# Token-mixing weights by row block, and a shorter pipeline for the first batch, in a fused retention and token-mixing kernel

## The chip, the cores and the metric

The kernel runs on one core of one Trainium2 chip. The metric is device time in microseconds. The core has five engines with an instruction stream each: TensorE (PE; its weight loads are listed as PEld), VectorE (DVE), ScalarE (ACT), GpSimd (POOL) and SyncE (SP, which only issues DMAs here). An engine works through its own stream in order and waits for others through semaphores.

## The reference

A retention recurrence over 8 heads, then a layer that mixes tokens with a phase and channels with a matrix:

```python
# q, k, v: [4, 8, 768, 64]
for t in range(S):
    state = gamma * state + outer(k[:, :, t], v[:, :, t])
    y[:, :, t] = scale * (q[:, :, t] @ state)
x = y with heads joined                      # [4, 768, 512]
theta = x @ w_theta
zr, zi = x * cos(theta), x * sin(theta)
u = x + w_tok_r @ zr + w_tok_i @ zi          # over the 768 tokens of a batch
out = u + maximum(u @ w_ch, 0)
```

All inputs and the output are float32; the two w_tok matrices are 768x768, w_theta and w_ch 512x512.

## The kernel before, in words

Tokens are cut into blocks of 128: six per batch, 24 chunks in all (number n = 6 * batch + c). The matmuls run in bf16. All code is emitted in one order by hand, and each engine takes its instructions in that order.

A chunk goes through these steps:

- **load_chunk** (L73): three DMAs on SP's queue, k, v, q, 256 KB each, into buffers kf, vf, qf (8 each).
- **att_prep** (L138, POOL): cast k to kb, scale q to qb and v to vb by powers of gamma.
- **T**, att_T (L151): eight PE transposes into kq_ps; DVE copies them to kqT.
- **A**, att_A (L162): eight PE matmuls k by q into at_ps; DVE multiplies by the causal mask into at.
- **Y**, att_Y (L180): PE matmuls of the running state with q (L186, for c > 0) and of at with vb (L192) into yT_ps, and the state update st_ps (L200, for c < 5). ACT copies yT_ps to xT and the state to stbd.
- **X**, att_X (L215): PE transposes xT back (x_ps, copied by DVE to x_sb) and multiplies by w_theta (th_ps, L226); ACT takes cosine and sine into cs.
- **Z**, att_Z (L234): DVE multiplies cs with x_sb into z.

A token block m of a batch needs z of all six chunks of that batch:

- **M**, moe_M (L241): twelve 512-wide matmuls of the transposed token weights wT with z into y_ps, in two halves; after the second, DVE adds x_sb into u.
- **U**, moe_U (L256): four transposes of u, which ACT copies to uT.
- **O**, moe_O (L264): four 512-wide matmuls with w_ch into o_ps, DVE's final maximum and sum into ot, and the output DMA on SP's queue.

The weights are prepared on the way: w_theta is cast by ACT (wth), w_ch by POOL (wch), and **w_tok** (L274) takes one block of 128 rows of w_tok_r or w_tok_i: a cast on POOL to wrow (3 buffers), six PE transposes into w_ps, and a copy into wT by DVE or ACT. There are twelve such blocks.

PSUM holds at_ps (two banks), st_ps (one), three buffers "acc" that yT_ps, th_ps, y_ps and o_ps take in turn, and two buffers "tr" that kq_ps, x_ps, u_ps and w_ps take in turn. A taker waits until the buffer's previous content has been copied out.

The order is a table of slots (L287 to L302). Chunk n starts in slot tau[n] and passes T, A, Y, X, Z in five successive slots, so five chunks are in flight. The chunks of batches 1 to 3 start three slots later than their number. Block m has M in slot mu[m], the first four slots after T of its batch's last chunk, and U and O in the slot behind. Within a slot the order is: loads, w_tok, att_prep of the next chunk, T, Z, U, first half of M, A, O, second half of M, Y, X (L304 to L344). The w_tok loads (L91, six buffers) are issued in slot 2, all of w_tok_r, then w_ch, then all of w_tok_i, ahead of the loads of chunk 6; the twelve w_tok run in slots 5 to 8, three per slot.

Of the kernel before, what the change touches and what calls it, by code (L numbers as in the profile page):

```python
# [14 lines left out]
FT = mybir.dt.float32  # L15
BF = mybir.dt.bfloat16
# [16 lines left out]
def kernel(  # L33
# [17 lines left out]
    nc = tc.nc  # L51
    B, H, S, D = q.shape
    dm = H * D
    P = 128
    nT = S // P
    nD = dm // P
# [3 lines left out]
    NCH = B * nT  # L60
# [11 lines left out]

    def load_chunk(n):  # L73
        b, c = divmod(n, nT)
        for name, src in (("kf", k), ("vf", v), ("qf", q)):
            t = io.tile([P, H, D], FT, name=name, bufs=8)
            nc.sync.dma_start(  # L77
                out=t, in_=src[b, :, c * P:(c + 1) * P, :].rearrange("h s d -> s h d"))
            raw[n, name] = t

    wdma = {}

    def load_w512(name, src):
        t = io.tile([P, nD, dm], FT, name="w512", bufs=1)
        nc.sync.dma_start(out=t, in_=src.rearrange("(a p) e -> p a e", p=P))
        wdma[name] = t

    def load_wtok(r, t0):
        src = (moe_w_tok_r, moe_w_tok_i)[r]
        t = io.tile([P, S], FT, name="wtok", bufs=6)  # L90
        nc.sync.dma_start(out=t, in_=src[t0 * P:(t0 + 1) * P, :])  # L91
        wdma[r, t0] = t

    load_chunk(0)
    load_chunk(1)
    load_w512("th", moe_w_theta)
    for n in range(2, 6):
        load_chunk(n)


    posn = const.tile([P, nT], FT)
# [17 lines left out]
    ident = const.tile([P, P], BF)  # L119
# [6 lines left out]
    for i in range(2):  # L126
        t = const.tile([P, NP, P], BF, name=f"stbd{i}")
# [3 lines left out]
    wth = const.tile([P, nD, dm], BF)  # L131
    wch = const.tile([P, nD, dm], BF)
# [5 lines left out]
    def att_prep(n):  # L138
        c = n % nT
        r3 = "p (h d) -> p h d"  # L140
        kb = work.tile([P, dm], BF, name="kb", bufs=4)
        qb = work.tile([P, dm], BF, name="qb", bufs=3)
        vb = work.tile([P, dm], BF, name="vb", bufs=4)
        nc.gpsimd.tensor_copy(kb.rearrange(r3, h=H), raw[n, "kf"])  # L144
        nc.gpsimd.tensor_mul(qb.rearrange(r3, h=H), raw[n, "qf"],  # L145
                             _bcast_last(qsc[:, c], D))
        nc.gpsimd.tensor_mul(vb.rearrange(r3, h=H), raw[n, "vf"],  # L147
                             _bcast_last(vsc[:, c], D))
        st[n] = dict(kb=kb, qb=qb, vb=vb)

    def att_T(n):  # L151
        s = st[n]
        kq_ps = psum.tile([P, 2 * NP, P], BF, name="kq_ps", tag="tr", bufs=2)
        for i, src in enumerate((s["kb"], s["qb"])):
            for j in range(NP):
                nc.tensor.transpose(kq_ps[:, i * NP + j, :],  # L156
                                    src[:, j * P:(j + 1) * P], ident)
        kqT = work.tile([P, 2 * NP, P], BF, name="kqT", bufs=4)
        nc.vector.tensor_copy(kqT, kq_ps)  # L159
        s["kqT"] = kqT  # L160

    def att_A(n):  # L162
        s = st[n]
        kqT = s["kqT"]
        at_ps = psum.tile([P, 2, NP, P], FT, name="at_ps", tag="at", bufs=1)
        for j in range(NP):
            for par in range(2):
                rows = slice(par * D, (par + 1) * D)
                nc.tensor.matmul(at_ps[:, par, j, :], kqT[rows, j, :],  # L169
                                 kqT[rows, NP + j, :], start=(j == 0),  # L170
                                 stop=(j == NP - 1), skip_group_check=True)
        at = work.tile([P, 2, NP, P], BF, name="at", bufs=2)
        nc.vector.tensor_mul(at.rearrange("p a j t -> p (a j) t"),  # L173
                             at_ps.rearrange("p a j t -> p (a j) t"),
                             _bcast_mid(mask, H))
        s["at"] = at
# [57 lines left out]
    def att_Z(n):  # L234
        b, c = divmod(n, nT)
        nc.vector.tensor_mul(zs[b][:, c], st[n]["cs"], _bcast_mid(xs[b][:, c, :], 2))  # L236
# [1 line left out]

    mo = {}

    def moe_M(m, half):  # L241
        b, t0 = divmod(m, nT)
        if half == 0:
            mo[m] = dict(y=psum.tile([P, dm], FT, name="y_ps", tag="acc", bufs=3))
        y_ps = mo[m]["y"]
        for s0 in range(half * 3, half * 3 + 3):
            for r in range(2):
                nc.tensor.matmul(y_ps, wT[r][:, s0, t0 * P:(t0 + 1) * P],  # L248
                                 zs[b][:, s0, r, :], start=(s0 == 0 and r == 0),
                                 stop=(s0 == nT - 1 and r == 1))  # L250
        if half == 1:
            u = work.tile([P, dm], BF, name="u", bufs=3)
            nc.vector.tensor_add(u, y_ps, xs[b][:, t0, :])  # L253
            mo[m]["u"] = u

    def moe_U(m):  # L256
        u_ps = psum.tile([P, nD, P], BF, name="u_ps", tag="tr", bufs=2)
        for j in range(nD):
            nc.tensor.transpose(u_ps[:, j, :], mo[m]["u"][:, j * P:(j + 1) * P], ident)  # L259
        uT = work.tile([P, nD, P], BF, name="uT", bufs=2)  # L260
        nc.scalar.copy(uT, u_ps)  # L261
        mo[m]["uT"] = uT

    def moe_O(m):  # L264
        b, t0 = divmod(m, nT)
        o_ps = psum.tile([P, dm], FT, name="o_ps", tag="acc", bufs=3)
        for j in range(nD):
            nc.tensor.matmul(o_ps, mo[m]["uT"][:, j, :], wch[:, j, :], start=(j == 0),  # L268
                             stop=(j == nD - 1))
        ot = work.tile([P, dm], FT, name="ot", bufs=4)  # L270
        nc.vector.scalar_tensor_tensor(ot, o_ps, 0.0, mo[m]["u"], ALU.max, ALU.add)  # L271
        nc.sync.dma_start(out=out[b, t0 * P:(t0 + 1) * P, :], in_=ot)

    def w_tok(r, t0):  # L274
        row = work.tile([P, S], BF, name="wrow", bufs=3)
        nc.gpsimd.tensor_copy(row, wdma[r, t0])
        w_ps = psum.tile([P, nT, P], BF, name="w_ps", tag="tr", bufs=2)
        for s0 in range(nT):
            nc.tensor.transpose(w_ps[:, s0, :], row[:, s0 * P:(s0 + 1) * P], ident)
        dst = wT[r][:, :, t0 * P:(t0 + 1) * P]  # L280
        if t0 % 2:
            nc.scalar.copy(dst, w_ps)
        else:
            nc.vector.tensor_copy(dst, w_ps)


    tau = {}  # L287
    for n in range(NCH):
        tau[n] = n if n < nT else n + 3
    mu = {}  # L290
    for m in range(B * nT):
        b = m // nT
        ready = tau[b * nT + nT - 1] + 4
        mu[m] = max(ready, mu.get(m - 1, 0) + 1)
    stage = {}
    for n in range(NCH):
        for off, f in enumerate("TAYXZ"):
            stage[f, tau[n] + off] = n
    for m in range(B * nT):
        stage["M", mu[m]] = m  # L300
        stage["O", mu[m] + 1] = m
    last = mu[B * nT - 1] + 1  # L302

    att_prep(0)  # L304
    for slot in range(last + 1):
        g = lambda f: stage.get((f, slot))
        if slot == 0:
            nc.scalar.copy(wth, wdma["th"])
        if slot == 2:
            for r in range(2):  # L310
                for t0 in range(nT):
                    load_wtok(r, t0)
                if r == 0:
                    load_w512("ch", moe_w_ch)
            for n in range(6, 8):
                load_chunk(n)
        if slot == 7:
            nc.gpsimd.tensor_copy(wch, wdma["ch"])
        if slot > 2 and slot + 5 < NCH:
            load_chunk(slot + 5)  # L320
        if 5 <= slot < 9:
            for i in range((slot - 5) * 3, (slot - 4) * 3):
                w_tok(i // nT, i % nT)
        nxt = stage.get(("T", slot + 1))
        if nxt is not None:
            att_prep(nxt)
        if g("T") is not None:
            att_T(g("T"))
        if g("Z") is not None:
            att_Z(g("Z"))  # L330
        if g("O") is not None:
            moe_U(g("O"))
        if g("M") is not None:
            moe_M(g("M"), 0)
        if g("A") is not None:
            att_A(g("A"))
        if g("O") is not None:
            moe_O(g("O"))
        if g("M") is not None:
            moe_M(g("M"), 1)  # L340
        if g("Y") is not None:
            att_Y(g("Y"))
        if g("X") is not None:
            att_X(g("X"))  # L344


# [28 lines left out]
```

## Time and profile before

| | before |
|---|---|
| time, median of 3 runs | 202.91 us (202.55 to 203.26) |
| profiled execution: time | 203.53 us |
| profiled execution: span | 201.8 us |
| PE busy | 168.5 us (83%) |
| PEld busy | 94.9 us (47%) |
| DVE busy | 108.7 us (54%) |
| ACT busy | 79.0 us (39%) |
| POOL busy | 78.9 us (39%) |

Two numbers need care. A PE matmul row lists the whole passage of a matmul through the array (379 ns for a 512-wide one), while successive ones start about 216 ns apart; so work on PE is counted from start to start. And shares of busy time are means over stages that have different limits. The span begins with the first instruction and ends with the last.

### The profile page before, as it was taken

Reading aid. Unit: us, or ns where it says so; the run is one execution under the profiler, and the core shown is the slowest. Engines: PE = TensorE matmul, PEld = TensorE weight load, DVE = VectorE, ACT = ScalarE, POOL = GpSimd, SP = SyncE. Lnnn points to the kernel's source line nnn. Section 1 sums busy time; section 2 is a strip of 40 time slices with the busy share of each in tenths; the row PEclk is TensorE's granted clock in tenths of the full one; section 3 lists DMA queues with packets and bytes.
Section 4 is the critical chain, followed back from the end, with each engine's and each line's share of the span. In section 5 each row is a group of like instructions: output and inputs, shape, how many; then the busy total and the mean of one; then the engine's idle time right before and its main releaser. Section 6 shows DMA issues by size and latency. Waiting matters only on the chain.

```text
span 201.8 us, 3699 instructions
## 1 busy us (share of the span) xinstructions
PE 168.5 (83%) x1456; PEld 94.9 (47%) x1480; DVE 108.7 (54%) x153; ACT 79.0 (39%) x147; POOL 78.9 (39%) x105
## 2 busy tenths in 40 slices
PE   0235786898999999799999999999999999877872
PEld 0123544665445655565565555555555444333330
DVE  1133453775565677679667766676557434233221
ACT  3031482687113433576543454335544343111110
POOL 4555859689855427585536452225000000000000
PEclk9999998799999999999999999999999999999999
DMA  6999999999999999999999111100111001112111
GB/s 143 245 284 218 221 356 394 400 203 233 220 175 229 221 213 255 253 258 260 231 228 235 61 52 55 52 28 27 52 55 52 28 25 55 52 62 83 64 52 52
DMA packets 81137, 32.22 MB, mean 160 GB/s; under 512 B 75488, under 2 KB 75488, under 8 KB 81120
## 3 DMA queue, kind: packets, MB, share of 16 engines
q1 hardware_dynamic: 81120, 31.99, 68.7%
q8 instruction: 11, 0.18, 0.4%
q14 instruction: 6, 0.05, 0.1%
HBM read 25.69 MB, written 6.29 MB: 158 GB/s over the span
## 4 chain that ended last, share of the span: by engine, by line
PE 70%; SPq 10%; ACT 5%; DVE 5%; DMA 3%; issue 3%; POOL 2%; ACTq 0%; POOLq 0%
PE y_ps L248 29%; PE o_ps L268 11%; SPq L77 10%; PE th_ps L226 9%; PE yT_ps L192 4%; PE kq_ps L156 3%; DMA qf<-in_q_dram 3%; PE at_ps L169 3%; PE u_ps L259 3%; DVE u L253 3%; PE st_ps L200 3%; PE x_ps L223 3%; PE yT_ps L186 2%; ACT cs L231 2%; ACT cs L230 1%
## 5 line engine op out<-in xcount | busy, mean ns | idle before, releaser
L248 PE MATMUL y_ps<-z,wti 128*128 128x512 bf16 x144 | 54.6, 379 | 0.9
L248 PE MATMUL y_ps<-z,wtr 128*128 128x512 bf16 x127 | 48.1, 379 | 0.0
L206 ACT CAST xT<-yT_ps 128x512 bf16<-128x512 f32 x24 | 14.1, 586 | 62.8 <-PE yT_ps L192 62.7
L159 DVE COPY kqT<-kq_ps 128x1024 bf16<-128x1024 bf16 x24 | 16.6, 690 | 30.1 <-PE kq_ps L156 30.1
L173 DVE TENSOR_TENSOR at<-at_ps,mask 128x1024 bf16<-128x1024 f32 x24 | 29.3, 1221 | 6.4 <-PE at_ps L169 6.4
L147 POOL TENSOR_TENSOR vb<-vf,vsc 128x512 bf16<-128x512 f32 x24 | 26.4, 1099 | 13.9 <-PE st_ps L200 7.8
L145 POOL TENSOR_TENSOR qb<-qf,qsc 128x512 bf16<-128x512 f32 x24 | 25.0, 1043 | 12.6 <-DMA qf<-in_q_dram 12.6
L144 POOL CAST kb<-kf 128x512 bf16<-128x512 f32 x24 | 15.8, 657 | 30.0 <-PE st_ps L200 26.4
L268 PE MATMUL o_ps<-wch,uT 128*128 128x512 bf16 x94 | 24.4, 381 | 2.9 <-ACT uT L261 2.7
L271 DVE SCALAR_TENSOR_TENSOR ot<-o_ps,u 128x512 f32<-128x512 f32 x24 | 16.5, 685 | 18.6 <-PE o_ps L268 18.2
L261 ACT COPY uT<-u_ps 128x512 bf16<-128x512 bf16 x24 | 14.1, 586 | 31.4 <-PE u_ps L259 31.4
L226 PE MATMUL th_ps<-wth,xT 128*128 128x512 bf16 x91 | 24.3, 388 | 0.7 <-issue 0.4
L236 DVE TENSOR_TENSOR z<-cs,x_sb 128x1024 bf16<-128x1024 bf16 x24 | 18.7, 781 | 8.8 <-ACT cs L231 8.7
L253 DVE TENSOR_TENSOR u<-y_ps,x_sb 128x512 bf16<-128x512 f32 x24 | 16.6, 692 | 11.3 <-PE y_ps L248 11.2
L248 PEld LDWEIGHTS <-wtr 128*128 128x128 bf16 x144 | 14.1, 98 | 14.1
L248 PEld LDWEIGHTS <-wti 128*128 128x128 bf16 x144 | 14.1, 98 | 14.0
L230 ACT ACTIVATE cs<-th_ps,halfpi 128x512 bf16<-128x512 f32 x24 | 16.5, 687 | 10.5 <-PE th_ps L226 10.4
L156 PE MATMUL kq_ps<-ident,kb 128*128 128x128 bf16 x96 | 10.4, 238 | 8.2 <-POOL kb L144 8.0
L156 PE MATMUL kq_ps<-ident,qb 128*128 128x128 bf16 x96 | 10.6, 241 | 6.9 <-POOL qb L145 6.9
L231 ACT ACTIVATE cs<-th_ps,zerob 128x512 bf16<-128x512 f32 x24 | 16.3, 680 | 0.0
L211 ACT CAST stbd<-st_ps 64x256 bf16<-64x256 f32 x40 | 14.7, 366 | 0.4
L156 PEld LDWEIGHTS <-kb 128*128 128x128 bf16 x96 | 7.8, 106 | 13.4 <-POOL kb L144 8.6
(44 smaller groups left out, 165.4 us busy)
## 6 DMA issues: line engine op xcount, KB each, us to landing
kf<-in_k_dram SPq DMA_DIRECT2D x24, 256.0 KB, 4.8
vf<-in_v_dram SPq DMA_DIRECT2D x24, 256.0 KB, 5.1
qf<-in_q_dram SPq DMA_DIRECT2D x24, 256.0 KB, 5.2
out_dram<-ot SPq DMA_DIRECT2D x24, 256.0 KB, 2.0
wtok<-in_moe_w_tok_r_dram SPq DMA_DIRECT2D x6, 384.0 KB, 6.6
wtok<-in_moe_w_tok_i_dram SPq DMA_DIRECT2D x6, 384.0 KB, 7.1
w<-in_moe_w_theta_dram SPq DMA_DIRECT2D x1, 1024.0 KB, 6.6
w<-in_moe_w_ch_dram SPq DMA_DIRECT2D x1, 1024.0 KB, 9.3
```

What stands on the lines that cost most here:

```text
L77: nc.sync.dma_start(out=t, in_=src[b, :, c * P:(c + 1) * P, :].rearrange("h s d -> s h d"))
L145: nc.gpsimd.tensor_mul(qb.rearrange(r3, h=H), raw[n, "qf"], _bcast_last(qsc[:, c], D))
L147: nc.gpsimd.tensor_mul(vb.rearrange(r3, h=H), raw[n, "vf"], _bcast_last(vsc[:, c], D))
L156: nc.tensor.transpose(kq_ps[:, i * NP + j, :], src[:, j * P:(j + 1) * P], ident)
L173: nc.vector.tensor_mul(at.rearrange("p a j t -> p (a j) t"), at_ps.rearrange("p a j t -> p (a j) t"), _bcast_mid(mask, H))
L226: nc.tensor.matmul(th_ps, s["xT"][:, j, :], wth[:, j, :], start=(j == 0), stop=(j == NP - 1))
L230: nc.scalar.activation(cs[:, 0, :], th_ps, AF.Sin, bias=halfpi, scale=1.0)
L231: nc.scalar.activation(cs[:, 1, :], th_ps, AF.Sin, bias=zerob, scale=1.0)
L236: nc.vector.tensor_mul(zs[b][:, c], st[n]["cs"], _bcast_mid(xs[b][:, c, :], 2))
L248: nc.tensor.matmul(y_ps, wT[r][:, s0, t0 * P:(t0 + 1) * P], zs[b][:, s0, r, :], start=(s0 == 0 and r == 0), stop=(s0 == nT - 1 and r == 1))
L253: nc.vector.tensor_add(u, y_ps, xs[b][:, t0, :])
L268: nc.tensor.matmul(o_ps, mo[m]["uT"][:, j, :], wch[:, j, :], start=(j == 0), stop=(j == nD - 1))
```

## The change

The table of slots goes. The program is written as a part for the six chunks of batch 0 and a loop for the rest.

- Loads: within a chunk q goes before v. kf, qf, vf have nine buffers, w512 two, wtok four. Behind the loads of chunks 0 to 5 come row block 0 of both token weights, w_ch, chunk 6, and then in turn a pair of row blocks (1 to 5) and a chunk (7 to 11), then chunk 12.
- w_tok now takes a pair, the real and the imaginary block t0; DVE copies the real one, ACT the imaginary one. Pair 0 stands behind the six chunks of batch 0, pair m + 1 in the slot of block m.
- The pipeline is shorter: Y of a chunk follows A in the same slot, X one slot later, Z two slots later. In batch 0 the order of an iteration is T(n), Y(n-1), A(n), X(n-1), Z(n-2).
- M of block 0 starts ahead of Y and X of chunk 5. Blocks of batch 0 then run in the slots of chunks 6 to 11, the slot of chunk 12 has no M, and blocks from 6 on run in the slots of chunks 13 and up.
- Within a slot: loads, T, Z, att_prep, first half of M, U of the block before, A, second half of M, O of the block before, Y, w_tok, X.

```diff
-        for name, src in (("kf", k), ("vf", v), ("qf", q)):
-            t = io.tile([P, H, D], FT, name=name, bufs=8)
+        for name, src in (("kf", k), ("qf", q), ("vf", v)):
+            t = io.tile([P, H, D], FT, name=name, bufs=9)
...
-        t = io.tile([P, nD, dm], FT, name="w512", bufs=1)
+        t = io.tile([P, nD, dm], FT, name="w512", bufs=2)
...
-        t = io.tile([P, S], FT, name="wtok", bufs=6)
+        t = io.tile([P, S], FT, name="wtok", bufs=4)
...
-    for n in range(2, 6):
+    for n in range(2, nT):
         load_chunk(n)
+    load_wtok(0, 0)
+    load_wtok(1, 0)
+    load_w512("ch", moe_w_ch)
+    load_chunk(nT)
+    for t0 in range(1, nT):
+        load_wtok(0, t0)
+        load_wtok(1, t0)
+        load_chunk(nT + t0)
+    load_chunk(2 * nT)
...
-    def w_tok(r, t0):
...
+    def w_tok(t0):
+        for r in range(2):
+            row = work.tile([P, S], BF, name="wrow", bufs=3)
+            nc.gpsimd.tensor_copy(row, wdma[r, t0])
+            w_ps = psum.tile([P, nT, P], BF, name="w_ps", tag="tr", bufs=2)
+            for s0 in range(nT):
+                nc.tensor.transpose(w_ps[:, s0, :], row[:, s0 * P:(s0 + 1) * P], ident)
+            dst = wT[r][:, :, t0 * P:(t0 + 1) * P]
+            if r:
+                nc.scalar.copy(dst, w_ps)
+            else:
+                nc.vector.tensor_copy(dst, w_ps)
...
+    for n in range(nT):
+        att_T(n)
+        if n == 1:
             nc.scalar.copy(wth, wdma["th"])
+        if n > 0:
+            att_Y(n - 1)
+        att_A(n)
+        if n > 0:
+            att_X(n - 1)
+        if n > 1:
+            att_Z(n - 2)
+        if n + 1 < nT:
+            att_prep(n + 1)
+    w_tok(0)
+    nc.gpsimd.tensor_copy(wch, wdma["ch"])
+    att_Z(nT - 2)
+    moe_M(0, 0, 3)
+    att_Y(nT - 1)
+    att_X(nT - 1)
+    att_Z(nT - 1)
...
+    for i, (n, m) in enumerate(slots):
+        if n is not None and n + 5 < NCH and n >= nT + 2:
+            load_chunk(n + 5)
+        if n is not None:
+            att_T(n)
+        if prev2 is not None:
+            att_Z(prev2)
+        if i + 1 < len(slots) and slots[i + 1][0] is not None:
+            att_prep(slots[i + 1][0])
+        if m is not None and m > 0:
+            moe_M(m, 0, 3)
+        if prev_m is not None:
+            moe_U(prev_m)
+        if n is not None:
+            att_A(n)
+        if m is not None:
+            moe_M(m, 3, nT)
+        if prev_m is not None:
+            moe_O(prev_m)
+        if n is not None:
+            att_Y(n)
+        if m is not None and m + 1 < nT:
+            w_tok(m + 1)
+        if prev_n is not None:
+            att_X(prev_n)
+        prev2, prev_n, prev_m = prev_n, n, m
+    moe_U(prev_m)
+    moe_O(prev_m)
```

Three places in the order of the engines' streams. First SP's queue behind the loads of chunk 5, before:

```order
L91 DMA wtok<-in_moe_w_tok_r_dram 128x768 x6
L85 DMA w_213<-in_moe_w_ch_dram 128x4x512
L91 DMA wtok<-in_moe_w_tok_i_dram 128x768 x6
L77 DMA kf<-in_k_dram 128x8x64
L77 DMA vf<-in_v_dram 128x8x64
```

and now:

```order
L91 DMA wtok<-in_moe_w_tok_r_dram 128x768
L91 DMA wtok<-in_moe_w_tok_i_dram 128x768
L85 DMA w_114<-in_moe_w_ch_dram 128x4x512
L77 DMA kf<-in_k_dram 128x8x64
L77 DMA qf<-in_q_dram 128x8x64
L77 DMA vf<-in_v_dram 128x8x64
L91 DMA wtok<-in_moe_w_tok_r_dram 128x768
L91 DMA wtok<-in_moe_w_tok_i_dram 128x768
L77 DMA kf<-in_k_dram 128x8x64
```

Two row blocks instead of twelve stand ahead of chunk 6, and one chunk follows each pair.

Second VectorE's stream around M of block 0 (wtr is wT of the real weights). Before, from Z of chunk 5 on (z from cs_724):

```order
L159 COPY kqT_748<-kq_ps_739 128x1024
L236 TENSOR_TENSOR z_341<-cs_724,x_sb_340 128x1024
L253 TENSOR_TENSOR u_764<-y_ps_751,x_sb_340 128x512
L159 COPY kqT_787<-kq_ps_778 128x1024
L173 TENSOR_TENSOR at_812<-at_ps_803,mask_138 128x1024
```

and now, from the copy of block 0 on (z from cs_560 is chunk 4, from cs_619 chunk 5; kqT_638 is chunk 6; u_663 belongs to block 0):

```order
L294 COPY wtr_215<-w_ps_566 128x6x128
L245 TENSOR_TENSOR z_293<-cs_560,x_sb_292 128x1024
L237 COPY x_sb_292<-x_ps_608 128x512
L245 TENSOR_TENSOR z_293<-cs_619,x_sb_292 128x1024
L168 COPY kqT_638<-kq_ps_629 128x1024
L182 TENSOR_TENSOR at_655<-at_ps_646,mask_206 128x1024
L262 TENSOR_TENSOR u_663<-y_ps_586,x_sb_292 128x512
L294 COPY wtr_215<-w_ps_685 128x6x128
```

Z of chunk 5 has moved ahead of the copy kqT of chunk 6, and the mask product of chunk 6 stands between Z and u.

Third TensorE's stream in the last blocks, where no attention is left. Before, from the end of a block's M (y_ps_2565) on:

```order
L248 MATMUL y_ps_2565<-z_2058,wti_148 128x512
L259 LDWEIGHTS u_2586
L259 MATMUL u_ps_2588<-ident_133,u_2586 128x128
...
L248 LDWEIGHTS wtr_147
L248 MATMUL y_ps_2595<-z_2058,wtr_147 128x512
```

and now, from the end of the first half of the last block's M (y_ps_2588) on; u_2578 belongs to the block before it, so its u stands six matmuls back:

```order
L257 MATMUL y_ps_2588<-z_2013,wti_216 128x512
L268 LDWEIGHTS u_2578
L268 MATMUL u_ps_2595<-ident_201,u_2578 128x128
...
L257 LDWEIGHTS wtr_215
L257 MATMUL y_ps_2588<-z_2013,wtr_215 128x512
```

U of a block stood directly behind that block's M, and stands now behind the first half of the next block's M.

More of the change, by code (lines that the diff above doesn't have):

```diff
@@ L239, with moe_M @@
     mo = {}
-    def moe_M(m, half):
+    def moe_M(m, lo, hi):
         b, t0 = divmod(m, nT)
-        if half == 0:
+        if lo == 0:
             mo[m] = dict(y=psum.tile([P, dm], FT, name="y_ps", tag="acc", bufs=3))
         y_ps = mo[m]["y"]
-        for s0 in range(half * 3, half * 3 + 3):
+        for s0 in range(lo, hi):
             for r in range(2):
@@ L250, in moe_M @@
                                  stop=(s0 == nT - 1 and r == 1))
-        if half == 1:
+        if hi == nT:
             u = work.tile([P, dm], BF, name="u", bufs=3)
@@ L272, in moe_O @@
         nc.sync.dma_start(out=out[b, t0 * P:(t0 + 1) * P, :], in_=ot)
-    def w_tok(r, t0):
[L275 to L284, printed above, removed]
@@ L287 @@
[L287 to L302, printed above, removed]
+    def w_tok(t0):
[10 more added lines that the diff above has]
+                nc.vector.tensor_copy(dst, w_ps)
@@ L304 @@
     att_prep(0)
-    for slot in range(last + 1):
-        g = lambda f: stage.get((f, slot))
-        if slot == 0:
+    for n in range(nT):
+        att_T(n)
+        if n == 1:
             nc.scalar.copy(wth, wdma["th"])
[L309 to L344, printed above, removed]
@@ new lines @@
+        if n > 0:
[14 more added lines that the diff above has]
+    att_Z(nT - 1)
+    slots = []
+    m = 0
+    for n in range(nT, NCH + 2):
+        b, c = divmod(n, nT)
+        slots.append((n if n < NCH else None,
+                      None if n == 2 * nT else m))
+        m += slots[-1][1] is not None
@@ new lines @@
+    while m < B * nT:
+        slots.append((None, m))
+        m += 1
+    prev_n, prev_m, prev2 = None, None, None
+    att_prep(nT)
+    for i, (n, m) in enumerate(slots):
[24 more added lines that the diff above has]
+        prev2, prev_n, prev_m = prev_n, n, m
```

## The prediction

> **What bounds the kernel now.** I read the page first, then stages of it, then the rows of TensorE.
>
> ```profile
> span 201.8 us, 3699 instructions
> PE   0235786898999999799999999999999999877872
> GB/s 143 245 284 218 221 356 394 400 203 233 220 175 229 221 213 255 253 258 260 231 228 235 61 52 55 52 28 27 52 55 52 28 25 55 52 62 83 64 52 52
> ```
>
> The profiled execution took 203.53 us, so 1.7 us lie around its span of 201.8. TensorE (PE) is thin in the first ten slices, full in the middle, thin again in the last six. What the change is worth stands in those two ends. The middle is TensorE's own pace, as one slot (chunk and token block side by side) shows:
>
> ```profile
> 111.48 0.39 PE L156 MATMUL kq_ps<-ident,kb 128*128 128x128 bf16 x4
> 111.93 0.39 PE L259 MATMUL u_ps<-ident,u 128*128 128x128 bf16 x4
> 113.55 0.40 PE L169 MATMUL at_ps<-kqT 64*128 64x128 bf16 x8
> 113.88 1.04 PE L268 MATMUL o_ps<-wch,uT 128*128 128x512 bf16 x4
> 114.75 0.38 PE L248 MATMUL y_ps<-z,wtr 128*128 128x512 bf16 x1
> 116.04 0.39 PE L186 MATMUL yT_ps<-kqT,stbd 128*128 128x128 bf16 x4
> 116.71 0.40 PE L200 MATMUL st_ps<-vb,kb 128*128 128x128 bf16 x4
> 116.94 0.39 PE L223 MATMUL x_ps<-ident,xT 128*128 128x128 bf16 x4
> 118.03 0.39 PE L156 MATMUL kq_ps<-ident,kb 128*128 128x128 bf16 x4
> ```
>
> The first column is the start, and no row names an idle time. From start to start: T (the L156 transposes) 0.45, U and the first half of M 1.62, A 0.33, O 0.87, the second half of M 1.29, Y 0.67 and its state update 0.23, X 1.09. Together 118.03 - 111.48 = 6.55 us. Reordering within such a slot can gain nothing.
>
> At the back end there is a hole:
>
> ```profile
> 166.00:202.00 36.00, 26.23 (x138) 11.50 (x137) 10.85 (x17) 5.26 (x9) 0.00 (x0) 0.99 0.16 59
> 177.38 0.40 PE L259 MATMUL u_ps<-ident,u 128*128 128x128 bf16 x4 [0.79 <-DVE u L253]
> 178.91 1.03 PE L268 MATMUL o_ps<-wch,uT 128*128 128x512 bf16 x4
> 180.85 0.38 PE L248 MATMUL y_ps<-z,wti 128*128 128x512 bf16 x1
> 182.02 0.40 PE L259 MATMUL u_ps<-ident,u 128*128 128x128 bf16 x4 [0.79 <-DVE u L253]
> 195.18 0.69 DVE L253 TENSOR_TENSOR u<-y_ps,x_sb 128x512 bf16<-128x512 f32 x1 [0.60 <-PE y_ps L248]
> ```
>
> In the stage 166 to 202 PE is busy 26.2 of 36 us. A block without attention takes 182.02 - 177.38 = 4.64 us, but its work ends at 180.85 plus one 512-wide pace of 0.22, so it is 3.69 us. The other 0.95 us is U's wait for VectorE's u (0.69 us long).
>
> At the front end PE waits for data:
>
> ```profile
> 20.70 1.33 SPq L77 DMA_DIRECT2D vf<-in_v_dram  x1
> 22.07 1.14 SPq L77 DMA_DIRECT2D qf<-in_q_dram  x1
> 35.81 0.43 SPq L77 DMA_DIRECT2D kf<-in_k_dram  x1
> 28.67 1.04 POOL L145 TENSOR_TENSOR qb<-qf,qsc 128x512 bf16<-128x512 f32 x1 [2.40 <-DMA qf<-in_q_dram]
> 30.66 4.75 POOL L276 CAST wrow<-wtok 128x768 bf16<-128x768 f32 x6
> 37.20 1.90 POOL L318 CAST wch<-w 128x2048 bf16<-128x2048 f32 x1 [1.80 <-DMA w<-in_moe_w_ch_dram]
> 49.27 0.38 PE L248 MATMUL y_ps<-z,wtr 128*128 128x512 bf16 x1
> ```
>
> Chunk 5 is complete only at 28.67, chunk 6 is not even asked for until 35.81, because all twelve w_tok loads stand before it in SP's queue, and the first token-mixing matmul runs at 49.27.
>
> **The change, stage 1: up to T of chunk 7.** Loads up to chunk 5 are the same bytes; only q now goes ahead of v, one issue step (22.07 - 20.70 = 1.4 us) sooner. Chunk 5's qb is then ready between 28.4 and the old 29.7. But PE has more behind it by then: in the new order T of chunk 5 stands behind A of chunk 4, Y of 3 and X of 2 and 3, 0.33 + 0.90 + 2 x 1.09 = 3.4 us that before came later. I put that T's end at 29.4, with 28.6 and 31 as ends.
>
> From there the chain is one of short waits. The durations:
>
> ```profile
> L206 ACT CAST xT<-yT_ps 128x512 bf16<-128x512 f32 x24 | 14.1, 586 | 62.8 <-PE yT_ps L192 62.7
> L230 ACT ACTIVATE cs<-th_ps,halfpi 128x512 bf16<-128x512 f32 x24 | 16.5, 687 | 10.5 <-PE th_ps L226 10.4
> L231 ACT ACTIVATE cs<-th_ps,zerob 128x512 bf16<-128x512 f32 x24 | 16.3, 680 | 0.0
> L282 ACT COPY wti<-w_ps 128x768 bf16<-128x768 bf16 x3 | 2.3, 806 | 0.0
> L159 DVE COPY kqT<-kq_ps 128x1024 bf16<-128x1024 bf16 x24 | 16.6, 690 | 30.1 <-PE kq_ps L156 30.1
> L236 DVE TENSOR_TENSOR z<-cs,x_sb 128x1024 bf16<-128x1024 bf16 x24 | 18.7, 781 | 8.8 <-ACT cs L231 8.7
> L173 DVE TENSOR_TENSOR at<-at_ps,mask 128x1024 bf16<-128x1024 f32 x24 | 29.3, 1221 | 6.4 <-PE at_ps L169 6.4
> ```
>
> - Y of chunk 4 to 30.3, A of 5 to 30.65, X of 4 (behind xT, 0.59) 30.8 to 31.9. The two row blocks' transposes, twice 0.33, to 32.6; their casts on POOL (0.8 each, 4.75 / 6) follow vb of chunk 5 and are done by 31.4.
> - On ACT the copy of the imaginary block stands behind both cs of chunk 4: 31.95 + 1.27 + 0.80 = 34.0. M(0), first half: to 35.15. Y of 5 to 35.8, wait for xT 0.65, X of 5 to 37.55, T of 6 to 38.0.
> - A of chunk 6 now waits longest: on VectorE kqT of 6 stands behind z of 5, which waits for cs of 5: 37.6 + 1.27, z 0.8, kqT 0.69, so 40.45; A to 40.8, M(0) second half to 42.1.
> - Y of 6 takes the accumulator buffer of M(0), so it waits for u (0.69): 42.85 to 43.4. Block 1's transposes to 44.2 (below).
>
> **Clock.** These waits leave PE mostly idle from 38.0 to 40.45, and before shows what may follow:
>
> ```profile
> 20.00:22.00 2.00, 0.98 (x12) 0.63 (x12) 0.17 (x1) 0.51 (x2) 1.92 (x2) 1.00 1.38 218
> 30.00:32.00 2.00, 0.46 (x6) 0.34 (x6) 0.00 (x0) 0.79 (x2) 2.00 (x3) 1.00 1.03 402
> 34.00:36.00 2.00, 2.00 (x26) 1.30 (x23) 1.66 (x4) 0.00 (x0) 1.40 (x2) 0.50 1.05 398
> 36.00:38.00 2.00, 1.78 (x15) 1.32 (x13) 1.50 (x2) 1.32 (x3) 0.80 (x1) 0.65 1.04 402
> ```
>
> The seventh number after the times is the granted clock: after PE was busy 0.46 of 2 us, it was 0.50 and 0.65 in the next busy stages, that is half rate for 2 + 1.4 = 3.4 us, a loss of 1.7 us of work. I charge 1.4 (part falls into waits), with 0 and 3.4 (twice over) as ends. [...] T of chunk 7 then starts at 44.2 + 1.4 = 45.6.
>
> **Do data arrive?** By the rates above (218 GB/s for chunks of 0.786 MB, 402 for whole rows): bytes up to chunk 5 are in by 26 to 28.5, then two row blocks, w_ch, chunk 6 at about 34.5 (wch's cast, 1.9 us, and chunk 6's three on POOL, 2.7 us, end by 37.7), blocks 1 by 37, chunk 7 at 41. POOL finishes vb of 7 at 42.1 and the two casts at 43.8, just ahead of PE: the 44.2 above. Per later slot 0.786 + 0.786 + 0.262 MB (the output) take at those rates 3.6 + 2.0 + 1.2 = 6.8 us against 7.55 us of PE. SP is held at pair 3 until POOL has cast pair 1, and the chunk loads queue behind it; that loop spans two slots, its issue (4.2) + landing (about 5) + POOL's five operations (4.4) make 13.6, or 6.8 us per slot. Both fit, by 0.7 us.
>
> **Stage 2: slots of chunks 7 to 23.** 17 x 6.55 = 111.4. Added: four pairs of block transposes, 4 x 0.66, each with about 0.35 us until VectorE's copy frees the buffer for X, 4.0 in all; 0.4 once for block 1's copy. Taken off: slot 12 has no M (2.6), slot 13 no U and O (1.1), chunk 5 of three batches no state update (0.7), chunk 0 of two no L186 (0.6). Slot 12 without M has little cover: A waits 0.5 for kqT, Y 0.4 for at. Sum 111.7: to 157.3.
>
> **Stage 3: tail.** U of the block before now stands behind the next first half of M (1.29 us), which covers u (0.69), and O behind the second half, which covers uT (0.59). Seven blocks at 3.69 and one X: 26.9, to 184.2. After the last M (its u starts at 195.18, 0.2 behind it) before needed 201.8 - 195.0 = 6.8 us; O of block 22 (0.86) now lies inside that. End 184.2 - 0.9 + 6.8 = 190.1, with the 1.7 around it 191.8. The profiled run is 0.6 above the median of the three, so 191.2 on that scale.
>
> As a check: when T of chunk 7 starts, 4.4 us of block transposes are still owed but A and Y of 6 (0.9) are done; before, that T began 2.6 us after 49.27. The front gives only 51.9 + 0.9 - 45.6 - 4.4 = 2.8 us. The rest, 8.9, is holes closed later, mostly in the tail. The front is the unsure part, the tail is not.
>
> **Rivals.**
> 1. The change doesn't do what it says at the front: the transposes are only moved, and the new waits (A of 6, Y of 6, block copies) eat the 2.8 us. 194.0. For it: the chain above is nearly all waits. Against: two of them are short by count. 0.15.
> 2. The clock stays at half from T of 5 to T of 7. That is 9.3 us of PE work by the steps above; doubled, and less the 1.4 charged, 199.1. For it: the 0.50 row. Against: the same rows show it back after 3.4 us of busy PE. 0.10.
> 3. Loads set the pace in slots 6 to 11. If rows go no faster than chunks (218 GB/s throughout), 1.835 MB take 8.4 us, 6 x 0.87 more: 196.4. 0.10. The same mechanism ends **slower** where the rate falls under 193 GB/s: then a slot takes 9.5 us and six of them give back the 11.7. At 175, the lowest slice of the GB/s row while loads run (the first apart), a slot takes 10.5 and the end is 209. For it: in-order SP, four buffers, PE's transposes standing ahead of X. Against: that slice had no queue of loads. 0.03.
>
> **How the numbers follow.** Forecast 191.2, chance 0.62. Range 187.5 to 198: below, T of chunk 5 at its early end, no clock loss, and a block's copies free; above, rivals 1 and the first form of 3. A measurement here tells about 0.3% from no change. Faster 0.95 (all but the slower form and a fifth of rival 2), same 0.02, slower 0.03.
>
> **What would show it.** First token-mixing matmul near 34 instead of 49.27; T of chunk 7 between 44 and 47; slots of 7.5 then 6.55 us; tail blocks of 3.7 us without a wait for u. T of 7 later than 50, or slots 8 to 11 above 8 us with POOL waiting for wtok, would make the prediction wrong.

## The result and the profile after

| | before | after |
|---|---|---|
| time, median of 4 runs | 202.73 us (202.33 to 203.26) | 193.57 us (192.85 to 196.05) |
| ratio to before, 95% interval | 1 | 0.9544 (0.9498 to 0.9591) |
| profiled execution: time, span | 203.53 us, 201.8 us | 194.15 us, 192.4 us |

The run of 196.05 us was a disturbed one; the ratio leaves it out. The time falls by 9.2 us, where 11.7 were forecast. The page of after, with the rows of its slices (each 4.8 us):

```profile
span 192.4 us, 3717 instructions
PE 167.3 (87%) x1480; PEld 95.1 (49%) x1480; DVE 113.1 (59%) x153; ACT 80.2 (42%) x147; POOL 82.4 (43%) x105
PE   0447986757999999988999999999999999999982
GB/s 134 232 304 218 220 240 335 295 222 253 280 270 218 226 244 258 256 239 252 241 105 218 122 159 158 170 106 55 3 55 55 58 0 56 58 55 111 55 55 109
```

PE's work is the same (168.5 us before, 167.3 now); the sevens and eights of the tail have gone, and the thin front is shorter. The stretches of GB/s near 400 have gone too: row blocks and chunks now alternate.

The tail, in TensorE's timeline of after (start, length, work), two blocks without attention:

```profile
180.40 0.39 PE L268 MATMUL u_ps<-ident,u 128*128 128x128 bf16 x4
...
181.92 1.03 PE L277 MATMUL o_ps<-wch,uT 128*128 128x512 bf16 x4
184.07 0.39 PE L268 MATMUL u_ps<-ident,u 128*128 128x128 bf16 x4
185.38 0.38 PE L257 MATMUL y_ps<-z,wti 128*128 128x512 bf16 x1
```

U of a block runs at 180.40 and of the next at 184.07: 3.67 us per block against 4.64 before, and no row names a wait. The last M ends at 185.38 + 0.22, and the span 6.8 us later.

The front, in the same timeline:

```profile
33.20 0.39 PE L257 MATMUL y_ps<-z,wtr 128*128 128x512 bf16 x1 [0.58 <-DVE wtr L294]
37.32 0.39 PE L165 MATMUL kq_ps<-ident,kb 128*128 128x128 bf16 x4
40.17 0.40 PE L178 MATMUL at_ps<-kqT 64*128 64x128 bf16 x8 [2.24 <-DVE kqT L168]
44.32 0.51 PE L289 MATMUL w_ps<-ident,wrow 128*128 128x128 bf16 x6 [1.68 <-POOL wrow L286]
45.48 0.39 PE L165 MATMUL kq_ps<-ident,kb 128*128 128x128 bf16 x4
54.84 0.39 PE L165 MATMUL kq_ps<-ident,kb 128*128 128x128 bf16 x4
62.52 0.39 PE L165 MATMUL kq_ps<-ident,kb 128*128 128x128 bf16 x4
```

The first token-mixing matmul runs at 33.20 instead of 49.27. A of chunk 6 waits 2.24 us for kqT. Then pair 1's transposes (44.32) wait for POOL's casts, and T of chunk 7 starts at 45.48. The slot of chunk 7 takes 54.84 - 45.48 = 9.36 us, that of chunk 8 takes 7.68.

Why the casts are late stands in POOL's timeline:

```profile
40.44 0.61 POOL L153 CAST kb<-kf 128x512 bf16<-128x512 f32 x1 [2.06 <-DMA kf<-in_k_dram]
41.45 1.04 POOL L154 TENSOR_TENSOR qb<-qf,qsc 128x512 bf16<-128x512 f32 x1 [0.41 <-DMA qf<-in_q_dram]
42.46 1.04 POOL L156 TENSOR_TENSOR vb<-vf,vsc 128x512 bf16<-128x512 f32 x1
43.44 1.59 POOL L286 CAST wrow<-wtok 128x768 bf16<-128x768 f32 x2
```

Pair 1 was asked for ahead of chunk 7, but POOL takes its casts behind att_prep of chunk 7, so they wait for that chunk to land. And the slot of chunk 7 is long because of the clock; experiments 4 and 5 have that slot without the fall (stretches: length, busy time of PE, PEld, DVE, ACT, POOL with counts, granted clock, DMA share, GB/s):

```profile
38.00:40.00 2.00, 0.00 (x0) 0.00 (x0) 1.18 (x2) 0.79 (x2) 0.38 (x1) 1.00 1.03 182
42.00:44.00 2.00, 0.64 (x12) 0.38 (x12) 0.69 (x1) 1.21 (x3) 2.00 (x3) 1.00 1.01 339
46.00:48.00 2.00, 2.00 (x8) 0.78 (x7) 0.69 (x1) 0.44 (x1) 1.11 (x2) 0.50 1.13 219
48.00:50.00 2.00, 2.00 (x18) 0.97 (x16) 0.35 (x1) 0.58 (x1) 2.00 (x3) 0.72 1.01 348
```

PE is idle or nearly so in 38 to 40 and 42 to 44; the clock falls to 0.50 only afterwards, when PE is full again.

### The profile page after: what moved, and what is told of

It reads as the page before. It is cut to its first block, busy times and chain, and to the rows that moved or that the text cites. A ratio compares the mean times of both kernels' runs of the same rounds, so it can differ in the third digit from the quotient of the medians.

```text
span 192.4 us, 3717 instructions
## 1 busy us (share of the span) xinstructions
PE 167.3 (87%) x1480; PEld 95.1 (49%) x1480; DVE 113.1 (59%) x153; ACT 80.2 (42%) x147; POOL 82.4 (43%) x105
## 4 chain that ended last, share of the span: by engine, by line
PE 71%; SPq 17%; DMA 3%; DVE 2%; POOL 2%; issue 1%; ACT 1%; ACTq 0%; POOLq 0%
PE y_ps L257 32%; SPq L77 15%; PE o_ps L277 10%; PE th_ps L235 8%; PE kq_ps L165 4%; PE yT_ps L201 3%; DMA qf<-in_q_dram 3%; PE u_ps L268 3%; PE at_ps L178 3%; PE x_ps L232 3%; PE st_ps L209 2%; PE yT_ps L195 2%; SPq L91 2%; DVE wtr L294 1%; PE w_ps L289 1%
## 5 line engine op out<-in xcount | busy, mean ns | idle before, releaser
L257 PE MATMUL y_ps<-z,wtr 128*128 128x512 bf16 x144 | 55.6, 386 | 0.6 <-DVE wtr L294 0.6
L257 PE MATMUL y_ps<-z,wti 128*128 128x512 bf16 x144 | 55.4, 384 | 0.1
L156 POOL TENSOR_TENSOR vb<-vf,vsc 128x512 bf16<-128x512 f32 x24 | 29.9, 1248 | 1.0 <-DMA vf<-in_v_dram 0.7
L245 DVE TENSOR_TENSOR z<-cs,x_sb 128x1024 bf16<-128x1024 bf16 x24 | 21.3, 888 | 7.4 <-ACT cs L240 7.4
L235 PE MATMUL th_ps<-wth,xT 128*128 128x512 bf16 x96 | 25.5, 390 | 0.0
L237 DVE COPY x_sb<-x_ps 128x512 bf16<-128x512 bf16 x24 | 10.2, 423 | 10.5 <-PE x_ps L232 10.5
L277 PEld LDWEIGHTS <-uT 128*128 128x128 bf16 x96 | 9.2, 98 | 12.2 <-ACT uT L270 1.5
L178 PE MATMUL at_ps<-kqT 64*128 64x128 bf16 x192 | 10.0, 226 | 5.2 <-DVE kqT L168 5.2
```

What stands on the lines that cost most here:

```text
L156: nc.gpsimd.tensor_mul(vb.rearrange(r3, h=H), raw[n, "vf"], _bcast_last(vsc[:, c], D))
L235: nc.tensor.matmul(th_ps, s["xT"][:, j, :], wth[:, j, :], start=(j == 0), stop=(j == NP - 1))
L257: nc.tensor.matmul(y_ps, wT[r][:, s0, t0 * P:(t0 + 1) * P], zs[b][:, s0, r, :], start=(s0 == 0 and r == 0), stop=(s0 == nT - 1 and r == 1))
```

## Experiments

Each ran beside before on the same chip; the ratios are to before, with 95% intervals. Line numbers are those of each kernel's own file, so they can differ by a line or more.

**1. The tail alone undone, and done alone.** In the first kernel, after without its new order in slots that have only token blocks:

```diff
+        if n is None:
+            moe_U(prev_m)
         if m is not None and m > 0:
             moe_M(m, 0, 3)
-        if prev_m is not None:
+        if n is None:
+            moe_O(prev_m)
+        elif prev_m is not None:
             moe_U(prev_m)
```

(and O no more behind the second half there).

> The changed kernel with one thing undone: in the slots without a chunk, U of the block before stands ahead of the first half of M and O between the halves, as before the change. Theory (most of the gain is closed holes at the end): seven blocks wait again for u, 0.95 us each, so 6.6 us more than the changed kernel: about 200, ratio to before 0.987. Rival (the gain is the earlier start of the token mixing): no more than 1 us lost, 194.5, ratio 0.96.

Measured: 200.78 us, 0.9874 (0.9822 to 0.9926). In the second, before with nothing changed but that order, from slot 27 on:

```diff
+        tail = slot > 26
-        if g("O") is not None:
+        if g("O") is not None and not tail:
             moe_U(g("O"))
         if g("M") is not None:
             moe_M(g("M"), 0)
+        if g("O") is not None and tail:
+            moe_U(g("O"))
```

(and O likewise behind the second half).

> The kernel before with only that reorder: from slot 27 on, U behind the first half of M and O behind the second. Theory: nine blocks of 0.95 us at most, those of slots 27 to 29 less since they have attention beside them: 6 to 7.5 us less, about 196, ratio 0.967. Rival (the start is the gain): 201 or more, ratio over 0.99.

Measured: 196.35 us, 0.9677 (0.9629 to 0.9726). The first kernel's timeline of TensorE in the tail:

```profile
178.78 0.40 PE L268 MATMUL u_ps<-ident,u 128*128 128x128 bf16 x4 [0.79 <-DVE u L262]
183.42 0.40 PE L268 MATMUL u_ps<-ident,u 128*128 128x128 bf16 x4 [0.79 <-DVE u L262]
```

The same place in the second's:

```profile
178.81 0.39 PE L259 MATMUL u_ps<-ident,u 128*128 128x128 bf16 x4
182.49 0.39 PE L259 MATMUL u_ps<-ident,u 128*128 128x128 bf16 x4
```

4.64 us per block with the old order, 3.68 with the new one, whichever the front. Undone, the tail costs 0.9874 - 0.9544 = 3.3%, or 6.7 us; alone it brings 3.2%, or 6.6. So the two ends add up: some 6.6 us of the 9.2 are the tail, and 0.9677 - 0.9544 = 1.3%, about 2.7 us, are all the rest. The intervals reach about 0.5% to each side, so the 1.3% is good to some 0.7%, or 1.4 us.

**2. Loads by row blocks or rows first.** After, with all twelve row blocks and w_ch ahead of chunk 6, and all six pairs prepared ahead of the first M:

```diff
-    load_wtok(0, 0)
-    load_wtok(1, 0)
-    load_w512("ch", moe_w_ch)
-    load_chunk(nT)
-    for t0 in range(1, nT):
+    for t0 in range(nT):
         load_wtok(0, t0)
         load_wtok(1, t0)
+        if t0 == 2:
+            load_w512("ch", moe_w_ch)
+    for t0 in range(nT):
         load_chunk(nT + t0)
...
-    w_tok(0)
+    for t0 in range(nT):
+        w_tok(t0)
```

(six wtok buffers instead of four, and no w_tok in the later slots).

> The changed kernel with all twelve row blocks (and w_ch among them) loaded ahead of chunk 6, and all six pairs prepared ahead of M of block 0; six wtok buffers. Theory: the block-wise loading gives nearly nothing by itself, since the transposes (4.4 us with their waits) are only moved and chunk 6 comes about 9 us later: T of chunk 7 near 50.5 with nothing owed, against 45.5 with 4.4 owed and 1.7 of half clock; 192 to 195, ratio 0.955. Rival (loading by block is what pays): T of chunk 6 nine us later costs most of these nine, 200 or more, ratio 0.985 or more.

Measured: 199.59 us, 0.9844 (0.9792 to 0.9895). My theory fell: this is 3.0% or 6 us slower than after. TensorE's timeline, and then a stage of it (columns as above):

```profile
40.06 0.82 PE L288 MATMUL w_ps<-ident,wrow 128*128 128x128 bf16 x6 [3.37 <-POOL wrow L285]
...
56.49 0.39 PE L164 MATMUL kq_ps<-ident,kb 128*128 128x128 bf16 x4
```

```profile
36.00:48.00 12.00, 7.46 (x47) 4.74 (x48) 3.54 (x5) 3.19 (x4) 7.89 (x9) 0.50 1.04 309
```

The short pipeline has no more chunks to work on by then, so PE waits 3.37 us for rows, runs at half clock throughout these 12 us, and T of chunk 7 starts at 56.49, 11 us later than in after (with all block transposes done, 4.4 us of them).

So that it isn't the early transposes that cost, a second kernel changes the order of the loads only (twelve wtok buffers to allow it, and seven of kf, qf and vf to make room); every w_tok stays in its slot.

> The changed kernel with only the order of loads changed: all twelve row blocks (twelve wtok buffers, seven instead of nine for k, q and v) ahead of chunk 6, the pairs still prepared one per slot. It tells apart why all rows first cost 6 us. Theory (TensorE starves: ten more row blocks, 3.9 MB at about 400 GB/s, put chunk 6 back by 9 to 10 us, so T of 6 comes near 46 or 47 and T of 7 near 52 to 54 with four pairs still owed): 199 to 202, ratio 0.98 to 0.995. Rival (what cost was preparing all pairs before M of block 0, not the arrival of chunk 6): 193 to 195, ratio under 0.96.

Measured: 201.2 us, 0.9874 (0.9782 to 0.9966), as the theory had it. T of chunk 6 now waits for chunk 6:

```profile
45.73 0.61 PE L164 MATMUL kq_ps<-ident,kb 128*128 128x128 bf16 x4 [8.06 <-POOL kb L152]
```

It starts at 45.73, in after at 37.32. The granted clock fell during this wait (0.89 from 38 to 42) and was 0.50 from 42 to 50, so the 3.3% by which this kernel is slower than after are the late chunk and the slow clock together.

**3. Loads by row blocks with the long pipeline.** The long pipeline of before with the reordered tail, and all that after has besides (order of loads, buffers, pairs, q ahead of v):

```diff
-        if slot == 2:
-            for r in range(2):
-                for t0 in range(nT):
-                    load_wtok(r, t0)
...
-        if 5 <= slot < 9:
-            for i in range((slot - 5) * 3, (slot - 4) * 3):
-                w_tok(i // nT, i % nT)
+        if slot == 8:
+            w_tok(0)
+            nc.gpsimd.tensor_copy(wch, wdma["ch"])
...
+        m = g("M")
+        if m is not None and m + 1 < nT:
+            w_tok(m + 1)
```

> The long pipeline of before (its table of slots, five slots per chunk) with the reordered tail, and with the loads, buffers, pairs of row blocks and the order k, q, v of after; pair 0 is prepared in the slot before T of chunk 6, pair m + 1 in the slot of block m. It does what after does in all but the length of the pipeline at the front. Theory (at the front the loads by block are what pays, and the shorter pipeline only moves PE work that is owed in either case): the first token-mixing matmul near 35 to 36 us, 193 to 195 us, ratio 0.950 to 0.960, that is within 1.5 us of after. Rival (the loads by block pay only with the short pipeline, since the long one has too little other work for PE while it drains): no better than the long pipeline with the reordered tail alone, 196 to 198 us, ratio 0.967 or above.

Measured: 196.03 us, 0.9643 (0.9619 to 0.9667). The theory fell here too. The first token-mixing matmul ran at 39.02, the last of that block ended at 41.6, and then TensorE's timeline reads:

```profile
45.41 0.51 PE L289 MATMUL w_ps<-ident,wrow 128*128 128x128 bf16 x6 [3.63 <-POOL wrow L286]
46.79 0.63 PE L165 MATMUL kq_ps<-ident,kb 128*128 128x128 bf16 x4
```

In the five-slot pipeline A and Y of chunk 6 come only after T of chunk 7. So while chunk 7 and the casts behind it are on their way, PE has nothing to do for 3.63 us, where after still has A, half of M and Y of chunk 6. T of chunk 7 starts 1.3 us later than in after, with A and Y of chunk 6 (0.33 + 0.90) still owed: together about the 2.5 us by which the spans differ (194.9 and 192.4). Of these, only the 1.2 us still owed follow from the pipeline's length. In both kernels T of chunk 7 waits for POOL's casts; here they end at 46.12 and in after at 45.03, since POOL has chunk 7's k at 41.59 and not at 40.44. Why it came later isn't settled (in the control of experiment 5 it is 41.19). All four with the reordered tail:

| ratio to before | all rows ahead of chunk 6 | rows in pairs between chunks |
|---|---|---|
| long pipeline | 0.9677 | 0.9643 |
| short pipeline | 0.9844 (pairs prepared first), 0.9874 (pairs one per slot) | 0.9544 |

The loads by pairs alone bring 0.3%, which the intervals don't tell from nothing, and the short pipeline by itself loses. Only the two together pay.

**4. The casts of a pair ahead of att_prep.** The cast leaves w_tok and is issued before att_prep of the next chunk; four wrow buffers instead of three:

```diff
+    def w_cast(t0):
         for r in range(2):
-            row = work.tile([P, S], BF, name="wrow", bufs=3)
+            row = work.tile([P, S], BF, name="wrow", bufs=4)
             nc.gpsimd.tensor_copy(row, wdma[r, t0])
...
+        if m is not None and m + 1 < nT:
+            w_cast(m + 1)
         if i + 1 < len(slots) and slots[i + 1][0] is not None:
             att_prep(slots[i + 1][0])
```

> The changed kernel with the two casts of a row pair on POOL emitted ahead of att_prep of the next chunk instead of behind it (four wrow buffers instead of three). Theory (T of chunk 7 waits for the casts, which wait behind chunk 7's arrival): casts of pair 1 done near 40, its transposes near 42.6, T of 7 near 43.3 instead of 45.5, and if the shorter idle stretch keeps the clock up, 1.7 more: 2 to 4 us less, 190 to 191.5, ratio 0.94 to 0.947. Rival (PE's own chain sets T of 7): no change, 193.5, ratio 0.954.

Measured: 191.39 us, 0.9429 (0.9374 to 0.9484), and in its timeline of TensorE:

```profile
44.33 0.83 PE L296 MATMUL w_ps<-ident,wrow 128*128 128x128 bf16 x12
45.47 0.38 PE L165 MATMUL kq_ps<-ident,kb 128*128 128x128 bf16 x4 [0.31 <-DVE wtr L301]
53.35 0.39 PE L165 MATMUL kq_ps<-ident,kb 128*128 128x128 bf16 x4
```

No wait for POOL is left before the block transposes, and the slot of chunk 7 takes 7.88 us: the clock stayed at 1.00 from 34 to 50. T of chunk 7 is no earlier in this execution, because its front was late (T of chunk 5 at 29.80; in the control of experiment 5 it is at 28.0). Counted from T of chunk 6 it is: 45.47 - 38.86 = 6.61 us, against 45.48 - 37.32 = 8.16 in after. So the gain has two parts here, some 1.5 us from the wait for the casts and some 1.5 from the clock, of which this execution's late front took one back.

**5. The clock, and the control.** Idle time filled: nine matmuls, whose result nothing uses, ahead of A of chunk 6, and seven behind Y of chunk 6.

```diff
+        if i == 0:
+            idle_fill(9)
         if n is not None:
             att_A(n)
```

> The changed kernel with idle work on TensorE: nine 512-wide matmuls (identity by w_theta, result unused, 1.9 us) between T and A of chunk 6, where PE waited 2.24 us, and seven (1.5 us) between Y of chunk 6 and the transposes of pair 1, where it waited 1.68 us. Theory (the clock fell in the slot of chunk 7 because of these idle stretches, and that is worth 1.5 us): granted clock 1.00 from 44 to 50 us, slot of chunk 7 7.9 us long instead of 9.4, 1.5 less than the control, 192. Rival (the fall doesn't hang on these stretches or costs nothing): as the control or up to 0.5 us more.

And after again, on the same chip:

> The changed kernel itself once more, beside the next three. Every theory: 193 to 194, ratio 0.954.

Measured: 193.24 us, 0.9523 (0.9501 to 0.9545), and the control 193.73 us, 0.9542 (0.9502 to 0.9582). The filler kept the clock at 1.00 from 34 to 50, and its slot of chunk 7 took 8.05 us, but the time is the control's within the intervals; the theory's 1.5 us did not come. A stage of the control says why:

```profile
40.00:44.00 4.00, 3.06 (x17) 1.27 (x20) 1.85 (x3) 0.00 (x0) 2.51 (x3) 0.57 0.88 223
```

There the clock fell at once, in 40 to 44, where PE waits for the casts anyway. It still waited 0.35 us for them behind the fall, T of chunk 7 came at 46.12 (45.88 with the filler), and the slot of chunk 7 took 54.18 - 46.12 = 8.06 us. So a fall costs what lies behind it: nothing in the wait for casts, and 9.36 - 8.06 = 1.3 us where it came in the full slot after. These are two executions; where the clock fell in the control's other five runs isn't on record.

**6. The casts, and T of chunk 6 ahead of Z of chunk 5.** The kernel of experiment 4, and in addition the wait of 2.24 us shortened: att_prep and T of chunk 6 stand ahead of Z of chunk 5, so that VectorE copies kqT before it does z.

```diff
     att_X(nT - 1)
+    att_prep(nT)
+    att_T(nT)
     att_Z(nT - 1)
```

> The kernel with the casts ahead (191.4, ratio 0.943) and also att_prep and T of chunk 6 emitted ahead of Z of chunk 5, so that on VectorE kqT of 6 no longer stands behind z of 5. Theory (A of 6 waits 2.2 us for that order alone, and then T of 7 waits for qb of 7 instead): A of 6 about 1.8 us earlier, T of 7 about 1 us earlier, 190.4, ratio 0.938. Rival (chunk 7's arrival sets T of 7 already): no change, 191.4.

Measured: 189.74 us (189.68 to 189.92), 0.9344 (0.9327 to 0.9361), the best of all. Its timeline of TensorE:

```profile
37.84 0.40 PE L178 MATMUL at_ps<-kqT 64*128 64x128 bf16 x8 [0.79 <-DVE kqT L168]
42.08 0.38 PE L165 MATMUL kq_ps<-ident,kb 128*128 128x128 bf16 x4 [0.31 <-DVE wtr L301]
49.95 0.39 PE L165 MATMUL kq_ps<-ident,kb 128*128 128x128 bf16 x4
```

A of chunk 6 waits 0.79 us, T of chunk 7 starts 3.4 us earlier than in after, and its slot takes 7.87 us. From T of chunk 6, T of chunk 7 comes 5.63 us later, against 8.16 in after and 6.61 in experiment 4; the rest of the 3.4 us is an earlier front in this execution. The mean granted clock of the four runs is 0.999 to 1.000, the control's 0.988 to 0.998. The four runs also lie within 0.24 us, the control's within 2.4. That the clock alone explains this is not shown: experiment 4's runs have the same clock and lie 2 us apart.

**7. Slot 12 as well.** The kernel of 6 with X of chunk 11 between U and A in the slot that has no M:

> The same, and in the slot of chunk 12, which has no M, X of chunk 11 moved between U and A. Theory: X (1.09 us) covers A's wait for kqT (0.56) and the wait for uT (0.20), 0.7 us less than the one before, 189.7, ratio 0.934. Rival (cover lost elsewhere, as Y's wait for at stays at 0.5 and z of 11 comes no earlier): 0 to 0.3 less.

Measured: 189.87 us, 0.9351 (0.9327 to 0.9375): no gain that the intervals show. Its timeline there:

```profile
82.49 0.38 PE L232 MATMUL x_ps<-ident,xT 128*128 128x128 bf16 x4 [0.56 <-DVE kqT L168]
83.67 0.40 PE L178 MATMUL at_ps<-kqT 64*128 64x128 bf16 x8
85.97 0.39 PE L165 MATMUL kq_ps<-ident,kb 128*128 128x128 bf16 x4
```

X now has the wait that A had, since x_ps takes kq_ps' buffer and so needs kqT copied, but A behind it waits no more. The slot went from 5.85 to 4.87 us in the two profiles, but most of that is not X's move. The same slot with the same order takes 5.19 us in after and in the control. In experiment 6 it is longer by one wait:

```profile
83.52 0.41 PE L201 MATMUL yT_ps<-at,vb 128*64 128x128 bf16 x8 [1.15 <-DVE at L182]
```

In after this wait is 0.49 us. VectorE's z ahead of the mask product took 1.50 us in experiment 6, beside a scaling of v on POOL, and 0.84 in after (the last section comes back to this). So X's move is worth about 5.19 - 4.87 = 0.3 us, near the rival's bound, and the intervals can't show it. The front of this profile was 1.8 us later than that of experiment 6.

**8. q ahead of v.** After with the old order k, v, q:

> The changed kernel with only the order within a chunk's loads undone (k, v, q as before). Theory: qb of chunk 5 about 1.1 us later, T of 5 as much, but T of 7 waits for the casts of pair 1 behind chunk 7, whose last load lands at the same time: vb can follow qb at once, so 0.3 to 1.0 us more, 194 to 194.6, ratio 0.957. Rival (nothing waits for q early enough): 193.5, ratio 0.954.

Measured: 195.24 us, 0.9588 (0.9552 to 0.9625). POOL's timeline:

```profile
42.94 1.04 POOL L154 TENSOR_TENSOR qb<-qf,qsc 128x512 bf16<-128x512 f32 x1 [1.52 <-DMA qf<-in_q_dram]
```

qb of chunk 7 starts 1.49 us later than in after (41.45), as one more load stands ahead of it. The ratio is 0.4% higher, but the intervals overlap; the direction is as expected, and the size is not settled.

## Why the prediction was right, and by how much it was off

**The tail: right, in mechanism and size.** It was forecast that U behind half of the next M covers u. Blocks take 3.67 us against 3.69 forecast, and the last 6.8 us came as forecast. Experiment 1 shows it from both sides.

**T of chunk 7: the time right, the reason partly wrong.** 45.48 us against 45.6. The forecast had PE's own chain to 44.2, with the casts done at 43.8 just ahead of it, plus 1.4 of clock. In the trace PE had finished Y of chunk 6 by 42.5 and waited for the casts, done at 45.03. The step that failed is "POOL finishes ... the two casts at 43.8", read as no bound. Experiment 4 shows that the wait is the order on POOL: with the casts ahead, it is gone. Another wait that was charged did not occur: Y of chunk 6 was to wait for u, from 42.1 to 42.85, as the taker of M(0)'s buffer. It starts at 41.90, and u only at 42.01, so it did not wait for that buffer. With that, PE's chain up to the casts was about 0.9 us shorter than forecast. That the forecast 45.6 still met 45.48 is luck: the casts came 1.2 us later than forecast, and the 1.4 us of clock that were charged here did not fall here.

**The clock: charged in the right size, but in one place.** I put 1.4 us ahead of T of chunk 7. The fall is real, but its place varies: 40 to 44 in the control (0.57), under the wait for casts, and 46 to 50 in the profile of after (0.50, then 0.72), in a full slot. There the slot of chunk 7 took 9.36 us against 6.55 + 0.66 + 0.35 + 0.4 = 7.96 forecast.

What lets the clock fall, the runs do not show. In after it fell behind a wait of 2.24 us and one of 1.68 (granted clock 0.93 from 44 to 46, 0.50 from 46 to 48), in the control already behind the first wait of 2.24 us (0.64 from 40 to 42). The kernel of experiment 4 had a gap of 2.54 us ahead of A of chunk 6 and kept 1.00. So the length of the longest gap does not decide it, and my 1.4 us were an estimate from the rows of before alone.

**The end: 2.3 us late, and the sum closes.** The span was forecast at 190.1 us and is 192.4:

| term | forecast | profile of after | difference |
|---|---|---|---|
| T of chunk 7 starts | 45.6 | 45.48 | -0.1 |
| slot of chunk 7 | 7.96 | 9.36 | +1.4 |
| slots of chunks 8 to 10, each | 7.56 | 7.68 | +0.4 for three |
| slot 12 (6.55 - 2.6 - 0.3 + 0.9) | 4.55 | 5.19 | +0.6 |
| all the rest | | | 0.0 |

Slot 12 is a term that was mis-sized: its waits were put at 0.9 us. In TensorE's timeline they are these:

```profile
84.67 0.39 PE L268 MATMUL u_ps<-ident,u 128*128 128x128 bf16 x4
85.62 0.40 PE L178 MATMUL at_ps<-kqT 64*128 64x128 bf16 x8 [0.56 <-DVE kqT L168]
86.22 1.04 PE L277 MATMUL o_ps<-wch,uT 128*128 128x512 bf16 x4 [0.20 <-ACT uT L270]
87.75 0.41 PE L201 MATMUL yT_ps<-at,vb 128*64 128x128 bf16 x8 [0.49 <-DVE at L182]
```

The rows name 1.25 us, and from start to start it is more, as the named idle time is counted from the listed end of the row before: 84.67 + 0.39 = 85.06, and 0.56 later A starts. From start to start four transposes take 0.22 (those of T, from 84.22 to 84.44), so A starts 85.62 - 84.67 - 0.22 = 0.73 us late. Waits that I read as idle time were too small by that difference, 0.17 us here.

**The rivals.** The measured 193.57 us lie nearer to the first rival's 194.0 than to the forecast's 191.2, but the table above has the 2.3 us of the span mostly elsewhere: in the clock and in slot 12, behind T of chunk 7, and 0.4 in block copies. That the chain of waits eats the front's 2.8 us was half true: the waits at A of 6 and at the casts are there, that at Y of 6 is not, and T of 7 came on time. Half clock for the whole stretch did not happen in after; it did with rows first (0.50 from 36 to 48, experiment 2). Loads setting the pace shows in one place only, where PE waits behind chunk 7's arrival; from chunk 8 on, slots take 7.68 us, and POOL's wait for data (1.32 us for k of chunk 8, up to 46.36) is hidden.

**What the forecast didn't see:** that the change at the front is one thing, not two. I took the loads as data that do or don't arrive in time, and the pipeline as an order. Experiment 2 shows that the short pipeline, which has used up its six chunks early, needs chunk 6 early. Experiment 3 shows that the loads by pairs pay clearly only with the short pipeline; that it is the early work on chunk 6 accounts for about half of the difference, and the other half stays open.

## What to carry to other kernels

Count what PE still owes when it stops at a wait: a shorter pipeline brings work forward, and pays only if the next data come forward with it. An engine that converts data in order (POOL here) should take what is already there ahead of what is still to land; that was worth 1.1%, and with one copy moved ahead of one product 2%, in both cases together with the clock, which no longer fell. In a tail of dependent blocks, put the next block's first half between a result and its use.

## What the runs showed of the hardware

VectorE's z ran three times as long beside a cast on POOL (2.21 us against 0.68), which I had not priced. From the two timelines of after:

```profile
32.00 0.68 DVE L245 TENSOR_TENSOR z<-cs,x_sb 128x1024 bf16<-128x1024 bf16 x1
33.06 2.21 DVE L245 TENSOR_TENSOR z<-cs,x_sb 128x1024 bf16<-128x1024 bf16 x1
32.84 1.89 POOL L312 CAST wch<-w 128x2048 bf16<-128x2048 f32 x1 [1.96 <-DMA w<-in_moe_w_ch_dram]
```

The cast ends at 34.73, and 34.73 + 0.68 = 35.4, about where the long z ends (35.27): it looks as if z had waited for the cast to end and then run. That is a reading of these times; no row shows why. Where no POOL row overlaps it, z takes 0.68 to 0.69 us in after. Other runs have the two in other orders. In the filler's run of experiment 5 the same z ran from 32.40 to 33.09, ahead of the cast (33.32), and took 0.69 us, and the cast 1.90. In the control of that experiment z came first and the cast started while it ran:

```profile
33.49 0.68 DVE L245 TENSOR_TENSOR z<-cs,x_sb 128x1024 bf16<-128x1024 bf16 x1
33.78 2.14 POOL L312 CAST wch<-w 128x2048 bf16<-128x2048 f32 x1 [2.12 <-DMA w<-in_moe_w_ch_dram]
```

There z kept its 0.68 us, and the cast is the one that is longer, 2.14 us against 1.89. So in after and in the control the one that started second took longer, and the first did not. On the path of PE it cost 1.50 - 0.84 = 0.66 us in slot 12 of experiment 6: z there ran 1.50 us from 80.83, beside POOL's scaling of v from 80.74, and Y waited for the product behind it.

The row of granted clock doesn't show that TensorE is slow at the start: two matmuls 512 wide list 1.06 us at 16.67 and 0.60 at 83.79, though the granted clock is 1.00 in both stretches (16 to 18, and 82 to 86).

```profile
16.67 1.06 PE L235 MATMUL th_ps<-wth,xT 128*128 128x512 bf16 x2
83.79 0.60 PE L235 MATMUL th_ps<-wth,xT 128*128 128x512 bf16 x2
16.00:18.00 2.00, 2.00 (x10) 0.92 (x8) 0.42 (x1) 1.53 (x3) 1.69 (x3) 1.00 1.36 217
```
